# One core: features of phi(q) reordered, kv and M in groups of six heads, M's rows moved by DMA, and the first five tiles reordered

## The chip, the cores and the metric

The kernel runs on one core of one Trainium2 chip. The metric is the device time of one execution in microseconds (us). Before the change the median of three runs is 114.61 us (114.52 to 114.76). Engines are called as the profile calls them: PE (TensorE matmuls), PEld (its weight loads), DVE (VectorE), ACT (ScalarE), POOL (GpSimd), SP (SyncE, which issues most DMAs). `q`, `k`, `g` and `o` units are explained below.

## The reference, cut to what matters

```python
# S = 2048 tokens, D = 640 features, H = 32 heads of 20, F = 1536, C = 8; all bf16
xn = layernorm(x)                          # both branches read xn
# branch A: linear attention
q, k, v = split(xn @ wqkv)                 # per head: [S, 20]
phi = lambda t: where(t > 0, t + 1, exp(t)) + 1e-6
kv  = einsum("bhsd,bhse->bhde", phi(k), v) # per head 20 x 20
z   = sum over tokens of phi(k)
num = einsum("bhqd,bhde->bhqe", phi(q), kv)
den = phi(q) . z + 1e-6                    # one number per token and head
A   = (num / den) @ wo
# branch B: mixture of depths
r   = xn @ w_r;  idx = the 8 tokens with the largest r
y   = ((silu(xs @ w_gate) * (xs @ w_up)) @ w_down) * sigmoid(r[idx])   # xs = xn[idx]
B   = xn + scatter_add(idx, y)
out = x + A + B
```

## The kernel before

**Algebra.** v is never formed. With G = xn^T phi(k) (640 x 640), the kernel takes from wv^T G only the 20 x 20 blocks on the diagonal (that is kv, transposed), multiplies them by wo into one matrix M = blockdiag(kv) wo (640 x 640), and computes A = (phi(q) / den) M. The division is a multiplication of phi(q)^T (`pqT`, features on partitions, tokens along the row) by 1/den, which has to be spread from one row per head to the 20 rows of the head's features.

**Order.** All engines run an order written out by hand (`manual_schedule`): the order of the statements is the order on each engine's queue, and the framework only adds waits. 16 token tiles of 128 rows are used.

- *First five tiles* (L291 to L382): the mean and variance of tile t in two halves on DVE (`ln_stats`, L163, L166, L167), the inverse root on POOL (L169, L172; some 0.75 us, off DVE) or with root="A" as Ln and Exp on ACT (L176, L177), the scaling to xn on DVE (`ln_scale`, L181), five PE transposes (`turn_pe`, L193) and copies of the transposed tile out of PSUM (`turned`, L201 on ACT, L203 on DVE). Tiles 5 and later are transposed by DMA (`turn_dma`, L206). Seven matmuls on zeros and some short ones run ahead (`warm`, L292).
- *Loop over tiles 4 to 15* (L463 to L485): a k unit (`k_mm`, ten matmuls of 320 columns, L211), a q unit (`q_mm`, five matmuls of 512 columns, L245; 20 of them, unit u is feature chunk u mod 5 of 512 tokens) and a g unit (`g_mm`, five of 512 columns, L272). ACT takes Exp and Relu of each (`k_act` L227 to L229, `q_act` L257, L258), DVE joins them to phi (L234, L264). Weights and the x + xn store to a DRAM buffer (`xxd`) are issued by SP meanwhile.
- *Middle* (L492 to L783): z (L503), the top-8 search on DVE, the rest of G (`grest_mm`, L281), den of the first 1024 tokens (`den_mm`, L579; `den_act`, L590, L591), kv (`kv_mm`, L628: ten blocks of 64 columns, five matmuls each; masked by L640), M (`m_mm`, L655: four matmuls for each of five row chunks; copied by L666 or L668), the expert branch (`gu_mm` L693, L748, L756, ending in `y_sb`, L763, which POOL adds into `xxd` by an indirect DMA, L766), and the last seven q units. 1/den of the first half is written to DRAM (L620) and read back, each row 20 times, by 13 DMAs (`spread_dma`, L686); DVE multiplies five chunks of pqT by it (`scale_0`, L778). The sums x + xn + y come back by `reload` (L772).
- *Output stage* (L830 to L868): per token tile an o unit (`o_mm`, L810, ten matmuls of 320 columns over five feature chunks), `o_add` on DVE (L820) and a store (L827). Inside tiles 1 to 5 den of the second half is formed and spread on PE (`spread_mm`, L596: four matmuls for each of five chunks, in three places), copied by ACT (`spread_copy`, L610) and multiplied in by DVE (`scale_by`, L615).

PSUM has eight banks, given out by hand as the number in each call.

Of the kernel before, what the change touches and what calls it, by code (L numbers as in the profile page):

```python
# [21 lines left out]
NB = 10  # L22
EB = 80
DB = 64
# [13 lines left out]
def block_start(b):  # L38

    return DH * ((DB * b) // DH)  # L40


@with_exitstack
def kernel(
# [24 lines left out]
    evq = ctx.enter_context(tc.tile_pool(name="evq", bufs=2))  # L69
# [14 lines left out]
    wo_sb = sb([EB, NB, D], BF16, "wo_sb")  # L84
# [6 lines left out]
    grep = sb([P, D], BF16, "grep")  # L91
    headg = sb([P, KC, H], BF16, "headg")
# [11 lines left out]
    maskkv = sb([EB, 5, DB], BF16, "maskkv")  # L104
# [3 lines left out]
    kvT = sb([EB, NB, DB], BF16, "kvT")  # L108
# [3 lines left out]
    rdd = dram.tile([H, HALF], BF16, tag="rdd", name="rdd")  # L112
# [21 lines left out]
    nc.gpsimd.memset(grep[:], 1.0)  # L134

    def grep_rows(j, then=None):
        g = grep[32 * j : 32 * j + 32, :]
        nc.gpsimd.affine_select(
            out=g, in_=g, compare_op=ALU.is_ge, fill=0.0, base=0,
            pattern=[[1, D]], channel_multiplier=-DH,  # L140
        )
        if then is not None:
            then()
        nc.gpsimd.affine_select(
            out=g, in_=g, compare_op=ALU.is_ge, fill=0.0, base=DH - 1,
            pattern=[[-1, D]], channel_multiplier=DH,
        )
# [5 lines left out]
    grep_rows(0, late_x3)  # L153
# [88 lines left out]
    def q_mm(u, b, lo=0, hi=KC):  # L242
        m, tb = QU[u]
        for kc in range(lo, hi):
            nc.tensor.matmul(  # L245
                ps[:, b, :],
                lhsT=wq_sb[:, kc, m * P : (m + 1) * P],
                rhs=xnT[:, kc, tb * TBLK : (tb + 1) * TBLK],
                start=(kc == 0), stop=(kc == KC - 1),
            )  # L250
# [58 lines left out]
    warm(6, P)  # L309
# [3 lines left out]
    warm(4, P)  # L313
    turned(0, 7, "V", 0, 2)
    turned(0, 7, "A", 2, KC)
    ln_stats(2, "a")
# [6 lines left out]
    turned(1, 4, "A", 0, 2)  # L323
# [10 lines left out]
    ln_stats(2, "b")  # L334
    ln_stats(3)
    ln_scale(2)
    k_mm(1, 2, 0, 8)
    turn_pe(2, 7)
    k_mm(1, 2, 8)
# [3 lines left out]
    for b in range(5):  # L343
        nc.tensor.matmul(
            ps[0:EB, 4, b * DB : (b + 1) * DB],
            lhsT=grep[0:H, block_start(b) : block_start(b) + EB],
            rhs=grep[0:H, b * DB : (b + 1) * DB],
            start=(b == 0), stop=True, skip_group_check=True,
        )
    nc.scalar.copy(  # L350
        maskkv[:], ps[0:EB, 4, 0 : 5 * DB].rearrange("p (b f) -> p b f", b=5)
    )
    k_phi(0)
    k_mm(2, 5)
    ln_scale(3)
    turn_pe(3, 7)
    turned(3, 7, "A", 0, 2)
    turned(3, 7, "A", 2, KC)
    k_phi(1)
    g_mm(0)  # L360
    k_act(2, 5)
    ln_stats(4)
    ln_stats(5, "a")
# [3 lines left out]
    ln_stats(5, "b")  # L367
# [10 lines left out]
    ln_stats(7)  # L378
    ln_scale(6)
    turn_dma(6)  # L380
    q_mm(0, 7)
    k_phi(3)  # L382
    q_act(0, 7)

    def const_piece(i):
        if i == 0:
# [3 lines left out]
                pattern=[[P, KC], [-DH, H]], channel_multiplier=1,  # L390
            )
            nc.gpsimd.affine_select(
                out=headg[:], in_=headg[:], compare_op=ALU.is_ge, fill=0.0, base=DH - 1,
                pattern=[[-P, KC], [DH, H]], channel_multiplier=-1,
# [4 lines left out]
        elif i < 4:  # L399
            grep_rows(i)  # L400
# [37 lines left out]
    def load_wo(h):  # L438
        b0 = 5 * h
        src = bass.AP(  # L440
            tensor=A_wo.tensor, offset=A_wo.offset + HW * h * D,
            ap=[[D, EB], [3 * DH * D, 5], [1, D]],
        )
        nc.sync.dma_start(wo_sb[:, b0 : b0 + 5, :], src)
# [56 lines left out]
    def z_mm(t):  # L501
        for i in range(4):
            nc.tensor.matmul(  # L503
                ps[32 * i : 32 * i + 32, 6, 0 : KC * 32].rearrange("p (k f) -> p k f", k=KC),
                lhsT=ones_bf[:],
                rhs=pk[:, t, :].rearrange("p (k i f) -> p i k f", k=KC, i=4)[:, i, :, :],
                start=(t == 0), stop=(t == T - 1),
                tile_position=(0, 32 * i),
            )
# [21 lines left out]
    nc.scalar.copy(zs[:], ps[:, 6, 0 : KC * 32])  # L531
# [31 lines left out]
    for i in range(C):  # L563
# [5 lines left out]
        out=zm[:], in0=zT[:].rearrange("p (k h) -> p k h", k=KC), in1=headg[:], op=ALU.mult  # L569
# [24 lines left out]
    def spread_mm(h, m, half_bank):  # L594
        for j in range(4):
            nc.tensor.matmul(  # L596
                ps[:, j, 256 * half_bank : 256 * half_bank + 256],
                lhsT=grep[32 * j : 32 * j + 32, m * P : (m + 1) * P],
# [5 lines left out]
    spw = big.tile([P, 2, 4, 256], BF16, tag="wk_sb", name="spw")  # L604
    nsp = [0]

    def spread_copy(h, m, half_bank):
        w = spw[:, nsp[0] % 2, :, :]
        nsp[0] += 1
        nc.scalar.copy(w, ps[:, 0:4, 256 * half_bank : 256 * half_bank + 256])  # L610
        return w

    def scale_by(h, m, w):
        dst = pqT[:, m, h * HALF : (h + 1) * HALF].rearrange("p (j f) -> p j f", j=4)
        nc.vector.tensor_tensor(out=dst, in0=dst, in1=w, op=ALU.mult)  # L615
# [3 lines left out]
    for j in range(4):  # L619
        nc.sync.dma_start(  # L620
            rdd[:, 256 * j : 256 * j + 256], rdens[0][32 * j : 32 * j + 32, :]
        )

    def kv_mm(b0, b1, bank, base):
        for b in range(b0, b1):
            s0 = block_start(b)
            for c in range(KC):
                nc.tensor.matmul(  # L628
                    ps[0:EB, bank, (b - base) * DB : (b - base + 1) * DB],
                    lhsT=wv_sb[:, c, s0 : s0 + EB],  # L630
                    rhs=GT[:, c, b * DB : (b + 1) * DB],
                    start=(b == base and c == 0), stop=(c == KC - 1),
# [3 lines left out]
    def kv_mask(b0, b1, bank):  # L636
        b = b0
        while b < b1:
            e = min(b1, 5 * (b // 5) + 5)
            nc.vector.tensor_tensor(  # L640
                out=kvT[:, b:e, :],
                in0=ps[0:EB, bank, (b - b0) * DB : (e - b0) * DB].rearrange(
                    "p (b f) -> p b f", f=DB
                ),
                in1=maskkv[:, b % 5 : b % 5 + e - b, :], op=ALU.mult,
            )
            b = e
# [4 lines left out]
    def m_mm(m, b):  # L652
        for h in range(2):
            for j in range(2):
                nc.tensor.matmul(  # L655
                    ps[DB * j : DB * j + DB, b + h, 0:HW],
                    lhsT=kvT[:, 2 * m + j, :],
                    rhs=wo_sb[:, 2 * m + j, h * HW : (h + 1) * HW],
                    start=True, stop=True,
                    tile_position=(0, DB * j),  # L660
                )

    def m_copy(m, b, by_act=False):
        dst, src = M_sb[:, m, :].rearrange("p (b f) -> p b f", b=2), ps[:, b : b + 2, 0:HW]
# [4 lines left out]

    rsp = late[:, (T - 8) * D : (T - 8) * D + KC * HALF].rearrange("p (k f) -> p k f", k=KC)

    def spread_dma(m):
        f = m * P
        while f < (m + 1) * P:
            h, i = divmod(f, DH)
            n = ((m + 1) * P - f) // DH if i == 0 else 0
            if n:
# [217 lines left out]
```

## Time and profile before

| what | value |
|---|---|
| median of three runs | 114.61 us |
| the profiled execution's own time | 114.76 us |
| its span | 112.9 us |
| PE matmul busy | 106.7 us, 917 instructions |
| DVE busy | 84.6 us, 182 instructions |
| ACT busy | 59.3 us, 124 instructions |
| POOL busy | 32.1 us, 86 instructions |
| DMA | 23.25 MB, mean 206 GB/s |
| granted PE clock | 0.999 |

A row of the timeline gives start, duration, engine, source line, operation, output and inputs, shapes and count, and in brackets the idle time just before it with what ended it. A row of the chain of waits gives start, length and the engine and line that held the end of the program at that moment.

### The profile page before, as it was taken

How to read it: one execution, taken by the hardware profiler on the slowest of the kernel's cores; microseconds unless marked ns; L12 is line 12 of the kernel's file. 1: busy time of each engine (PE TensorE's matmuls, PEld its weight loads, DVE VectorE, ACT ScalarE, POOL GpSimd, SP SyncE). 2: the span in 40 equal slices, each digit the busy share in tenths (PEclk: the TensorE clock that was granted, in tenths of full speed). 3: DMA queues.
4: the chain of work that ended last, by engine and by line, in shares of the span. 5: the costliest groups of instructions: out<-in, count | busy, mean ns of one | idle time of the engine just before them, and what ended most of it. 6: DMA issues, size and time to landing. Idle time of an engine off the chain costs nothing.

```text
span 112.9 us, 2523 instructions
## 1 busy us (share of the span) xinstructions
PE 106.7 (94%) x917; PEld 63.6 (56%) x926; DVE 84.6 (75%) x182; ACT 59.3 (53%) x124; POOL 32.1 (28%) x86
## 2 busy tenths in 40 slices
PE   5999998999999999999999999999997999999990
PEld 2477563555555555555555589555334565777770
DVE  0787968988988898997888944348989568685580
ACT  1458819855686556865568542253885366300000
POOL 7405133278779788620000013100600000000000
PEclk9999999999999999999999999999999999999999
DMA  3999922324999969999972999023546927973333
GB/s 92 319 289 339 378 99 54 62 58 73 314 186 192 259 221 287 380 344 217 385 274 95 235 385 330 7 86 134 151 113 174 338 95 195 319 278 128 116 116 116
DMA packets 23410, 23.25 MB, mean 206 GB/s; under 512 B 8902, under 2 KB 21478, under 8 KB 23398
## 3 DMA queue, kind: packets, MB, share of 16 engines
q1 hardware_dynamic: 21420, 21.03, 64.8%
q10 hardware_dynamic: 1834, 2.02, 5.3%
q0 software_dynamic: 144, 0.04, 0.6%
q8 instruction: 7, 0.11, 0.4%
q14 instruction: 5, 0.04, 0.2%
HBM read 15.93 MB, written 5.35 MB: 189 GB/s over the span
## 4 chain that ended last, share of the span: by engine, by line
PE 86%; DVE 6%; issue 3%; ACT 2%; POOL 0%; ACTq 0%; DVEq 0%; POOLq 0%
PE ps L211 20%; PE ps L245 17%; PE ps L272 15%; PE ps L810 14%; PE ps L292 4%; PE ps L281 4%; DVE xn L820 2%; PE ps L628 2%; PE ps L693 2%; DVE pqT L778 1%; PE ps L193 1%; PE ps L655 1%; PE ps L579 1%; DVE pqT L264 1%; PE ps L503 1%
## 5 line engine op out<-in xcount | busy, mean ns | idle before, releaser
L211 PE MATMUL ps<-wk_sb,xnT 128*128 128x320 bf16 (+1 forms) x160 | 25.1, 300 | 0.0
L245 PE MATMUL ps<-xnT,wq_sb 128*128 128x512 bf16 x94 | 23.9, 379 | 0.9 <-ACT xnT L201 0.4
L810 PE MATMUL ps<-late,pqT 128*128 128x320 bf16 (+2 forms) x165 | 22.8, 295 | 0.6 <-DVE pqT L778 0.6
L211 PEld LDWEIGHTS <-xnT 128*128 128x128 bf16 x160 | 15.3, 98 | 8.6 <-issue 0.4
L272 PE MATMUL ps<-pk,xn 128*128 128x512 bf16 x77 | 19.7, 379 | 0.2
L810 PEld LDWEIGHTS <-pqT 128*128 128x128 bf16 x165 | 15.5, 98 | 7.4 <-DVE pqT L778 0.9
L227 ACT ACTIVATE ek<-ps 128x640 bf16<-128x640 f32 x16 | 11.3, 706 | 13.9 <-PE ps L211 13.9
L820 DVE TENSOR_TENSOR xn<-ps,x_sb 128x640 bf16<-128x640 f32 (+3 forms) x18 | 13.1, 747 | 6.0 <-PE ps L810 6.0
L257 ACT ACTIVATE eq<-ps 128x512 bf16<-128x512 f32 x20 | 12.3, 617 | 7.9 <-PE ps L245 7.8
L245 PEld LDWEIGHTS <-wq_sb 128*128 128x128 bf16 x100 | 9.3, 97 | 10.3 <-issue 1.7
L264 DVE SCALAR_TENSOR_TENSOR pqT<-eq,rq 128x512 bf16<-128x512 bf16 x20 | 13.7, 684 | 0.9 <-ACT rq L258 0.9
L234 DVE SCALAR_TENSOR_TENSOR pk<-ek,rk 128x640 bf16<-128x640 bf16 x16 | 12.9, 807 | 1.7 <-ACT rk L228 1.7
L272 PEld LDWEIGHTS <-xn 128*128 128x128 bf16 x80 | 7.6, 98 | 8.6
L258 ACT ACTIVATE rq<-ps 128x512 bf16<-128x512 f32 x20 | 12.3, 616 | 0.0
L181 DVE TENSOR_SCALAR xn<-x_sb,mv,rs 128x640 bf16<-128x640 bf16 x16 | 8.6, 536 | 3.9 <-POOL rs L172 3.6
L228 ACT ACTIVATE rk<-ps 128x640 bf16<-128x640 f32 x16 | 11.2, 702 | 0.0
L172 POOL TENSOR_TENSOR rs<-rs,half 128x1 f32<-128x1 f32 x14 | 10.7, 763 | 1.1
L169 POOL TENSOR_TENSOR rs<-mv,half 128x1 f32<-128x1 f32 x14 | 5.7, 409 | 15.6 <-DVE mv L167 15.5
L163 DVE BATCH_NORM_STATS2 st<-x_sb 128x6 f32<-128x320 bf16 x16 | 7.6, 472 | 3.2 <-DMA x_sb<-in_A_x_dram 3.2
L565 POOL COPY xsT<-xnT 128x5 bf16 x8 | 1.6, 206 | 21.6 <-DVE junk L714 18.1
L166 DVE BATCH_NORM_STATS2 st<-x_sb 128x6 f32<-128x320 bf16 x16 | 7.6, 475 | 0.0
L187 DVE TENSOR_TENSOR x_sb<-x_sb,xn 128x640 bf16<-128x640 bf16 x16 | 6.9, 477 | 0.0
(122 smaller groups left out, 101.1 us busy)
## 6 DMA issues: line engine op xcount, KB each, us to landing
x_sb<-in_A_x_dram SPq DMA_DIRECT2D x6, 320.0 KB
wg_sb<-in_B_w_gate_dram SPq DMA_DIRECT2D x5, 384.0 KB
wu_sb<-in_B_w_up_dram SPq DMA_DIRECT2D x5, 384.0 KB
wd_sb<-in_B_w_down_dram SPq DMA_DIRECT2D x3, 640.0 KB
xxd<-x_sb SPq DMA_DIRECT2D x2, 640.0 KB
out_dram<-xn SPq DMA_DIRECT2D x8, 160.0 KB
x_sb<-xxd SPq DMA_DIRECT2D x2, 640.0 KB
out_dram<-xn ACTq DMA_DIRECT2D x7, 160.0 KB
```

The source lines that it names most:

```text
L172: nc.gpsimd.tensor_tensor(out=rs[:, 1:2], in0=rs[:, 0:1], in1=half[:, 1:2], op=ALU.pow)
L211: nc.tensor.matmul(ps[:, b + h, 0:w], lhsT=xnT[:, kc, t * P : (t + 1) * P], rhs=wk_sb[:, kc, h * HW : h * HW + w], start=(kc == 0), stop=( ...
L227: nc.scalar.activation(e[:], ps[:, b : b + 2, 0:HW], AF.Exp)
L228: nc.scalar.activation(r[:], ps[:, b : b + 2, 0:HW], AF.Relu)
L234: nc.vector.scalar_tensor_tensor(out=pk[:, t, :].rearrange("p (b f) -> p b f", b=2), in0=e[:], scalar=1.0, in1=r[:], op0=ALU.min, op1=ALU.add,
L245: nc.tensor.matmul(ps[:, b, :], lhsT=wq_sb[:, kc, m * P : (m + 1) * P], rhs=xnT[:, kc, tb * TBLK : (tb + 1) * TBLK], start=(kc == 0), stop ...
L257: nc.scalar.activation(e[:], ps[:, b, :], AF.Exp)
L258: nc.scalar.activation(r[:], ps[:, b, :], AF.Relu)
L264: nc.vector.scalar_tensor_tensor(out=pqT[:, m, tb * TBLK : (tb + 1) * TBLK], in0=e[:], scalar=1.0, in1=r[:], op0=ALU.min, op1=ALU.add,)
L272: nc.tensor.matmul(ps[:, c, :], lhsT=xn[:, t, c * P : (c + 1) * P], rhs=pk[:, t, 0:512], start=(t == 0), stop=(t == T - 1),)
L810: nc.tensor.matmul(ps[:, b, 0 : c1 - c0], lhsT=pqT[:, kc, t * P : (t + 1) * P], rhs=M_sb[:, kc, c0:c1], start=(kc == 0), stop=(kc == KC - 1),)
L820: nc.vector.tensor_tensor(out=xn[:, t, c0:c1].rearrange("p (b f) -> p b f", f=w), in0=ps[:, b : b + n, 0:w], in1=x_sb[:, t, c0:c1].rearran ...
```

## The change

It has five parts.

1. **Features of phi(q).** The weights of q unit m were columns 128m to 128m+127 of wq; now they are columns 5p + m for p = 0 to 127, a view with a step of five elements. Row p of every chunk m then belongs to head p // 4, so one spread of 1/den (`gbig`, a 0/1 matrix) serves all five chunks. z is brought into the same order: its matmuls read contiguous columns, and the copy `zs` reorders them.
2. **The first half of the tokens** is divided like the second: `spread_mm(0)` (four matmuls) and one `spread_copy` of 1024 columns on ACT, then five multiplications. The DRAM detour (4 writes, 13 reads) is gone. For the second half there is one spread and one copy where there were five.
3. **kv and M** go by groups of six heads (five groups of 120 columns and one of 40): kv takes 30 matmuls (50 before), M 12 matmuls of up to 120 rows (20 of 64 rows in pairs before). The mask comes from POOL instead of five matmuls and an ACT copy in the first tiles.
4. **M's rows** must follow the order of the features, so each group is copied to `M_nat` (ACT four, DVE two) and one DMA on SP moves it: 120 rows go to 24 partitions with five rows each.
5. **First five tiles.** Tile 2's first half-statistics stand ahead of the copy of tile 0, its second half and an ACT root ahead of the copy of tile 1; tile 4's transposes stand behind k unit 3 with all of g unit 2 behind them; tile 5's statistics move behind them; two short warming matmuls go.

The diff, cut to its core:

```diff
-    warm(6, P)
+    warm(4, P)
     ln_scale(0)
     ln_stats(1, "b", root="A")
     turn_pe(0, 7)
     warm(4, P)
+    ln_stats(2, "a")
     turned(0, 7, "V", 0, 2)
     turned(0, 7, "A", 2, KC)
-    ln_stats(2, "a")
     ln_scale(1)
...
-    turned(1, 4, "A", 0, 2)
+    ln_stats(2, "b", root="A")
+    turned(1, 4, "V", 0, 2)
     turned(1, 4, "A", 2, KC)
...
-    ln_stats(2, "b")
-    ln_stats(3)
     ln_scale(2)
-    k_mm(1, 2, 0, 8)
+    ln_stats(3, "a")
+    k_mm(1, 2, 0, 4)
     turn_pe(2, 7)
-    k_mm(1, 2, 8)
+    k_mm(1, 2, 4)
...
-    for b in range(5):
-        nc.tensor.matmul(
-            ps[0:EB, 4, b * DB : (b + 1) * DB],
-            lhsT=grep[0:H, block_start(b) : block_start(b) + EB],
...
     k_mm(3, 5)
-    g_mm(2, 0, 3)
     turn_pe(4, 7)
-    g_mm(2, 3)
+    g_mm(2)
     turned(4, 7, "A", 0, 2)
     turned(4, 7, "A", 2, KC)
+    ln_stats(5)
     ln_scale(5)
...
-                lhsT=wq_sb[:, kc, m * P : (m + 1) * P],
+                lhsT=wq_sb[:, kc, :].rearrange("p (f m) -> p m f", m=KC)[:, m, :],
...
-    def spread_mm(h, m, half_bank):
+    def spread_mm(h):
         for j in range(4):
             nc.tensor.matmul(
-                ps[:, j, 256 * half_bank : 256 * half_bank + 256],
-                lhsT=grep[32 * j : 32 * j + 32, m * P : (m + 1) * P],
+                ps[:, j, 0:256],
+                lhsT=gbig[32 * j : 32 * j + 32, j * P : (j + 1) * P],
                 rhs=rdens[h][32 * j : 32 * j + 32, :],
...
+    def spread_copy(h):
+        nc.scalar.copy(spw[:, h, :, :], ps[:, 0:4, 0:256])
...
+    def kv_mm(g0, g1, bank):
+        for g in range(g0, g1):
+            f0, w = group(g)
             for c in range(KC):
                 nc.tensor.matmul(
+                    ps[0:w, bank, (g - g0) * GB : (g - g0) * GB + w],
+                    lhsT=wv_sb[:, c, f0 : f0 + w],
+                    rhs=GT[:, c, f0 : f0 + w],
...
+    def m_mm(g, b):
+        w = group(g)[1]
         for h in range(2):
+            nc.tensor.matmul(
+                ps[0:w, b + h, 0:HW],
+                lhsT=kvT[0:w, g, 0:w],
+                rhs=wo_sb[0:w, g, h * HW : (h + 1) * HW],
...
+    def m_out(g, b, by_act=False):
...
+        nc.sync.dma_start(M_sb[f0 // KC : (f0 + w) // KC, :, :], nat)
...
-    kv_mm(0, 8, 4, 0)
-    kv_mask(0, 8, 4)
-    for t in range(9, T):
+    kv_mm(0, 4, 4)
+    kv_mask(0, 4, 4)
+    for t in range(9, 11):
         grest_mm(t, 0, 4, 7)
+    spread_mm(0)
+    spread_copy(0)
+    for t in range(11, T):
+        grest_mm(t, 0, 4, 7)
...
-    for m in range(KC):
-        spread_dma(m)
...
-    MID = {1: den_1, 2: lambda: spread_1(0, 1), 4: lambda: spread_1(2, 3)}
-    END = {2: lambda: reload(8, 12), 4: lambda: reload(12, 16), 5: lambda: spread_1(4)}
+    MID = {1: den_1, 2: spread_1}
+    END = {2: lambda: reload(8, 12), 4: lambda: reload(12, 16)}
```

Three places show how instructions stand now. Names with a number are buffers of one tile: st, mv and rs hold statistics, mean with variance, and root; the pairs ek, rk and eq, rq hold Exp and Relu. Source lines differ by two to thirty between the kernels.

DVE in the first tiles, from the copy of tile 0's first two blocks on, before:

```order
L203 COPY xnT<-ps 128x2x128
L163 BN_STATS st_183<-x_sb 128x6
L181 TENSOR_SCALAR xn<-x_sb,mv_157,rs_158 128x640
L166 BN_STATS st_183<-x_sb 128x6
L167 BN_AGGR mv_184<-st_183 128x2
L163 BN_STATS st_220<-x_sb 128x6
L166 BN_STATS st_220<-x_sb 128x6
L167 BN_AGGR mv_221<-st_220 128x2
L181 TENSOR_SCALAR xn<-x_sb,mv_184,rs_185 128x640
```

and now, from tile 2's first half on:

```order
L161 BN_STATS st_180<-x_sb 128x6
L201 COPY xnT<-ps 128x2x128
L179 TENSOR_SCALAR xn<-x_sb,mv_158,rs_159 128x640
L164 BN_STATS st_180<-x_sb 128x6
L165 BN_AGGR mv_181<-st_180 128x2
L201 COPY xnT<-ps 128x2x128
L179 TENSOR_SCALAR xn<-x_sb,mv_181,rs_182 128x640
L161 BN_STATS st_220<-x_sb 128x6
```

Tile 2's statistics (st_183 before, st_180 now) have moved ahead of the copy out of bank 7, and tile 3's (st_220) behind tile 2's scaling; tile 1's first two blocks are now copied by DVE.

DVE between the expert branch's activations and the output stage, before (y_sb closes the expert branch):

```order
L750 COPY late<-ps 128x384
L264 SCALAR_TENSOR_TENSOR pqT<-eq_1267,rq_1268 128x512
L668 CAST late<-ps 128x640
L763 TENSOR_SCALAR y_sb<-ps,gcol 128x160
L668 CAST late<-ps 128x640
L264 SCALAR_TENSOR_TENSOR pqT<-eq_1336,rq_1337 128x512
L778 TENSOR_TENSOR pqT<-pqT,late 128x1024
L264 SCALAR_TENSOR_TENSOR pqT<-eq_1412,rq_1413 128x512
L778 TENSOR_TENSOR pqT<-pqT,late 128x1024
```

and now:

```order
L742 COPY late<-ps 128x384
L262 SCALAR_TENSOR_TENSOR pqT<-eq_1308,rq_1309 128x512
L754 TENSOR_SCALAR y_sb<-ps,gcol 128x160
L607 TENSOR_TENSOR pqT<-pqT,spw 128x1024
L262 SCALAR_TENSOR_TENSOR pqT<-eq_1377,rq_1378 128x512
L607 TENSOR_TENSOR pqT<-pqT,spw 128x1024
L262 SCALAR_TENSOR_TENSOR pqT<-eq_1388,rq_1389 128x512
L262 SCALAR_TENSOR_TENSOR pqT<-eq_1399,rq_1400 128x512
```

The copies of M are gone from this stretch, and of the five multiplications three stand ahead of it; the last one stood behind the last but one phi, and stands now behind the second.

ACT in the output stage, where the rows are the reciprocal of den (ld, rd), the stores that ACT issues and the copies of the spread, before:

```order
L590 ACTIVATE ld_1513<-ps,eps_100 128x256
L591 ACTIVATE rd_1514<-ld_1513 128x256
L827 DMA out_dram<-xn 128x640
L610 CAST spw<-ps 128x1024 x2
L827 DMA out_dram<-xn 128x640
L610 CAST spw<-ps 128x1024 x2
L827 DMA out_dram<-xn 128x640
L610 CAST spw<-ps 128x1024
```

and now:

```order
L588 ACTIVATE ld_1470<-ps,eps_100 128x256
L589 ACTIVATE rd_1471<-ld_1470 128x256
L805 DMA out_dram<-xn 128x640
L603 CAST spw<-ps 128x1024
L805 DMA out_dram<-xn 128x640 x6
L805 DMA out_dram<-xn 128x192
```

Four of five copies are gone, and with them the sixteen matmuls that fed them on PE.

More of the change, by code (lines that the diff above doesn't have):

```diff
@@ L617 @@
     den_mm(0, 6)
     den_act(0, 6)
[L619 to L626, printed above, removed]
+    def kv_mm(g0, g1, bank):
+        for g in range(g0, g1):
+            f0, w = group(g)
             for c in range(KC):
                 nc.tensor.matmul(
[L629 to L632, printed above, removed]
+                    ps[0:w, bank, (g - g0) * GB : (g - g0) * GB + w],
+                    lhsT=wv_sb[:, c, f0 : f0 + w],
+                    rhs=GT[:, c, f0 : f0 + w],
+                    start=(g == g0 and c == 0), stop=(c == KC - 1),
@@ L649, with kv_mask, kv_mask5 @@
+    def kv_mask(g0, g1, bank):
+        n = g1 - g0
+        nc.vector.tensor_tensor(
+            out=kvT[:, g0:g1, :],
+            in0=ps[0:GB, bank, 0 : n * GB].rearrange("p (g f) -> p g f", f=GB),
+            in1=mask2.unsqueeze(1).to_broadcast([GB, n, GB]), op=ALU.mult,
+        )
+    def kv_mask5(bank):
+        w = group(5)[1]
+        nc.vector.tensor_tensor(
+            out=kvT[0:w, 5, 0:w], in0=ps[0:w, bank, GB : GB + w], in1=mask2[0:w, 0:w],
+            op=ALU.mult,
+        )
     late = big.tile([P, T * D], BF16, tag="pk", name="late")
@@ L650 @@
     M_sb = late[:, 0 : KC * D].rearrange("p (k d) -> p k d", k=KC)
-    def m_mm(m, b):
+    M_nat = big.tile([P, KC, D], BF16, tag="wk_sb", name="M_nat")
+    def m_mm(g, b):
+        w = group(g)[1]
         for h in range(2):
[L654 to L661, printed above, removed]
```

243 lines of the change are left out of this document (103 added, 140 removed).

## The prediction

> **What bounds the kernel now.** I read the page's busy shares first, then the chain of waits in order of time, then the timeline at the places where the chain leaves PE.
>
> ```profile
> span 112.9 us, 2523 instructions
> PE 106.7 (94%) x917; PEld 63.6 (56%) x926; DVE 84.6 (75%) x182; ACT 59.3 (53%) x124; POOL 32.1 (28%) x86
> PE 86%; DVE 6%; issue 3%; ACT 2%; POOL 0%; ACTq 0%; DVEq 0%; POOLq 0%
> ```
>
> PE holds 86% of the chain. So the change is worth the PE time that it removes plus the PE waits that it ends, unless another engine takes over. The profiled execution took 114.76 us, its span is 112.9, and 1.86 us lie around it and stay. The median of the runs shown is 0.15 us lower, and I take that off at the end.
>
> The PE waits and the PE work that the change touches lie in three stretches. First tiles, in the chain:
>
> ```profile
> 10.39 0.30 PE ps L344 x5
> ...
> 16.70 0.29 PE ps L193 x5
> ...
> 17.01 0.76 ACT xnT L201 x2
> ...
> 19.06 1.51 PE ps L211 x10
> ```
>
> and one row of the timeline:
>
> ```profile
> 17.82 1.24 PE L245 MATMUL ps<-xnT,wq_sb 128*128 128x512 bf16 x5 [0.41 <-ACT xnT L201]
> ```
>
> L344 makes the mask. At 17.0 ACT empties bank 7 of tile 4, and q unit 0, which writes that bank, waits. From the first k unit of the loop (19.06) to the middle the chain stays on PE at 3.54 us a tile (k 1.38, q 1.08, g 1.08).
>
> Middle, chain:
>
> ```profile
> 25.19 1.08 PE ps L272 x5
> 26.27 1.38 PE ps L211 x10
> ...
> 67.33 1.65 PE ps L628 x40
> 68.98 2.46 PE ps L281 x44
> ...
> 73.44 0.50 PE ps L628 x10
> ...
> 74.87 0.39 PE ps L655 x4
> ...
> 79.82 1.19 PE ps L245 x5
> ```
>
> Output stage, chain, and one row of the timeline that shows the wait at its start:
>
> ```profile
> 86.90 0.99 PE L810 MATMUL ps<-late,pqT 128*128 128x320 bf16 x6 [0.58 <-DVE pqT L778]
> ```
>
> ```profile
> 86.90 0.99 PE ps L810 x6
> 87.89 0.66 PE ps L579 x20
> 88.55 1.47 PE ps L810 x10
> 90.02 0.33 PE ps L596 x8
> ...
> 95.96 0.29 PE ps L596 x4
> ```
>
> The first o unit waits for DVE's last multiplication of the first half. Later PE waits before the third spread (L596), whose banks the ACT copy of the second still holds.
>
> **Part A, first tiles.** Mask: 0.30 us of PE go. Its replacement on POOL runs inside the loop, where POOL has idle time. Bank 7: q unit 0 waited 0.41 us; behind the transposes stood two g matmuls of 0.22 us, now five (1.08 us by the row at 25.19), and ACT's copies need 0.76 us from the end of the transposes. 0.76 is under 1.08, so the wait goes. Sum -0.71.
>
> What the reordering could cost, by the rows of the same engines:
>
> ```profile
> 6.10 0.29 ACT L176 ACTIVATE rs<-mv,half 128x1 f32<-128x1 f32 x1 [1.11 <-DVE mv L167]
> 6.40 0.29 DVE L203 COPY xnT<-ps 128x256 bf16<-128x256 bf16 x1 [0.34 <-PE ps L193]
> 6.42 0.20 ACT L177 ACTIVATE rs<-rs 128x1 f32<-128x1 f32 x1
> 6.61 0.48 DVE L163 BATCH_NORM_STATS2 st<-x_sb 128x6 f32<-128x320 bf16 x1
> 8.09 0.75 ACT L201 COPY xnT<-ps 128x256 bf16<-128x256 bf16 x2 [0.77 <-PE ps L193]
> 8.74 0.71 ACT L227 ACTIVATE ek<-ps 128x640 bf16<-128x640 f32 x1
> ```
>
> DVE was idle for 0.34 us before the copy at 6.40. Half a set of statistics (0.48, some 0.1 of it overlapping the next) fits in with under 0.1 us left over, if tile 2 has landed by 6.0. At 6.61 it had, since no DMA wait stands there; so this costs 0 to 0.6, and I take 0. On ACT, Ln and Exp of tile 2's root now stand ahead of tile 1's copy. ACT was idle for 0.77 us there. Mean and variance are ready some 1.1 us after the scaling that begins near 6.7, at about 7.8; the root is done 0.5 later, at 8.3. ACT then copies three blocks, not five (DVE has the other two), and ends near 8.9, as now at 8.84. k unit 2 needs the banks of k unit 0 at 10.4, and the three ACT reads that begin then end at about 10.3. Queued behind the root on ACT are that copy and these reads, and k unit 1's second half waits for the copy only from 9.5. So the slack is 0.1 us, and I take no cost. DVE has the statistics of tiles 5 and 7 later than before, so that phi of tile 4 may come up to 0.4 us late for its g unit. Taken -0.7; bounds 0 to -0.85.
>
> **Part B, middle.** kv: 50 matmuls took 1.65 + 0.50 = 2.15 us, 0.041 each at 64 columns with weights of 80. Now 25 have 120 columns with weights of 120, and five 40 by 40. The nearest rows bound one of the 25: 0.056 (44 of 128 columns in 2.46) and 0.062 (0.041 times 120/80); five small ones at 0.041. 1.6 to 1.75, taken 1.7: -0.45. M: five units at 0.39 = 1.95 before, now 12 matmuls at the k unit's 0.138 = 1.66: -0.29. Spread of the first half on PE: half of the 0.33 that eight took, 0.17 to 0.33, taken 0.2. Sum -0.55.
>
> A rule speaks against this part. The Trainium skill (TensorE: Matmul & The Clock Gate, Weight-path perf modes) has the fast weight load only for weights of all 128 columns, and its section on LDWEIGHTS gives columns / 1.2 ns otherwise, 100 ns at 120 columns. If that were the pace, kv would take 2.7 us, Part B would come to about +0.45, and the whole to 112.5. The trace agrees that 80 columns load slower than 128, but not with the pace:
>
> ```profile
> L245 PEld LDWEIGHTS <-wq_sb 128*128 128x128 bf16 x100 | 9.3, 97 | 10.3 <-issue 1.7
> L628 PEld LDWEIGHTS <-wv_sb 128*80 128x80 bf16 x50 | 2.1, 120 | 0.5 <-issue 0.3 <-DMA wd_sb<-in_B_w_down_dram 0.2
> ```
>
> 120 ns for 80 columns stands against 97 ns for 128, yet the matmuls behind them went every 41 ns.
>
> Other engines in this stretch, by a row of the windows (stretch, length, then PE, PEld, DVE, ACT, POOL busy), one of the timeline and one of the groups:
>
> ```profile
> 71.44:76.79 5.35, 5.14 (x67) 2.44 (x69) 1.69 (x4) 2.82 (x6) 0.20 (x1) 1.00 0.20 61
> ```
>
> ```profile
> 75.16 0.56 DVE L744 TENSOR_TENSOR late<-ps,late 128x384 bf16<-128x384 f32 x1 [0.90 <-ACT late L742]
> ```
>
> ```profile
> L666 ACT CAST late<-ps 128x640 bf16<-128x640 f32 x2 | 1.4, 700 | 0.0
> ```
>
> ACT gains here one spread copy (1.01 us, in the row of L610 below), the GT copy that DVE had, and four copies of M at 0.70, two of which stand behind the expert branch's Exp; with 2.82 of 5.35 us busy it takes them in its idle time. DVE gains three multiplications (0.68, row L615 below) ahead of the expert product at 75.16; it was idle for 0.90 there and for most of the four us before, so y_sb, and with it the reload, stay at the same distance behind kv. SP has six DMAs in place of 4 + 13, behind the weights of w_down and ahead of the reloads. The last waits for ACT's copy of the last group, some 76.5 on the old clock, 8 us before the first o unit at 85. No row shows a DMA of this form; it costs nothing up to 8 us.
>
> **Part C, output stage.** Spread on PE: 0.33 + 0.33 + 0.29 = 0.95 before, once 0.2 now: -0.75. The second 0.33 is the spread of chunks 2 and 3, eight matmuls like the first. The wait at 86.90 (0.58, and 0.16 of refilling, since six matmuls took 0.99 and not 0.83) ends if DVE is no longer late. From 77 on DVE had seven phis, five multiplications, three copies of M; now seven phis and two multiplications. ACT is next: Exp and Relu of a q unit take 1.08 us start to start (84.20 to 85.28 below), as long as the unit on PE, so phi of the last unit ends some 2.0 us after PE has finished it; den needs it after one o unit and four matmuls (1.93 us) and four of its own five chunks (0.53): 0.45 us to spare. -0.74. The third spread's wait, 0.32 between the sixteen o matmuls' end at 95.64 and 95.96, goes with that spread. Sum -1.81.
>
> ```profile
> L610 ACT CAST spw<-ps 128x1024 bf16<-128x1024 f32 x5 | 4.9, 1014 | 3.7 <-PE ps L596 2.5 <-DVE xn L820 1.2
> L615 DVE TENSOR_TENSOR pqT<-pqT,spw 128x1024 bf16<-128x1024 bf16 x5 | 3.4, 682 | 0.9 <-ACT spw L610 0.9
> ```
>
> ```profile
> 84.20 0.60 ACT L257 ACTIVATE eq<-ps 128x512 bf16<-128x512 f32 x1 [0.49 <-PE ps L245]
> 84.41 2.33 SPq L772 DMA_DIRECT2D x_sb<-xxd  x5
> ...
> 85.28 0.60 ACT L257 ACTIVATE eq<-ps 128x512 bf16<-128x512 f32 x1
> ...
> 87.39 0.82 DVE L820 TENSOR_TENSOR xn<-ps,x_sb 128x640 bf16<-128x640 f32 x1
> ```
>
> DVE does one sum and one multiplication for each of tiles 2 to 6, 0.82 + 0.68 with some 0.14 of overlap, against 1.38 of PE: level.
>
> **The sum.** 114.76 - 0.70 - 0.55 - 1.81 = 111.7; less 0.15 for the median, 111.5 us.
>
> **Rivals.**
>
> *Strided weights (slower).* The q weights now step five elements, and no row of before has such a load. It took 97 ns, hidden behind a 216 ns matmul (1.08 / 5). There are 100 of them, so the 3.1 us gained are gone at 216 + 31 = 247 ns, 2.5 times the row. At three times (291) it is +7.5: 119 us. Against it: that is a long way from 97, and the slowest load in the rows, 120 ns for 80 columns, makes 192 for 128, still hidden. The Trainium skill (SBUF — State Buffer, The DMA port swizzle) lets bf16 step up to eight elements for free; no run here shows it.
>
> *The reload gates.* The reload was issued at 84.41, well behind the q units, and is as late on the new clock.
>
> ```profile
> 85.50:86.00 0.50, 0.50 (x6) 0.38 (x4) 0.50 (x2) 0.50 (x2) 0.00 (x0) 1.00 0.75 200
> 86.00:86.50 0.50, 0.33 (x3) 0.00 (x0) 0.50 (x2) 0.36 (x1) 0.00 (x0) 1.00 0.98 325
> ```
>
> The last number is GB/s: its bytes came from 85.5 on, so tile 0 landed near 86.5, at most by the sum at 87.39. On the old clock the third o unit wants that sum's bank at 87.7, and the sum takes 0.82. Landing at 87.39 costs 0.5: 112.0.
>
> *The first tiles give nothing.* Part A falls to 0 because DVE's or ACT's queue holds the next tile up as much as the bank did: 112.2.
>
> *Slow 120-column loads.* If a matmul of kv went at the 120 ns of the row above: 3.6 us against 1.7, 113.4.
>
> **How the numbers follow.** The forecast 0.60 (own range 110.8 to 112.1), first tiles give nothing 0.17, reload 0.10, slow loads 0.05, strided weights 0.08. All but the last are faster: a measurement here tells 0.2% (0.23 us) from no change, and only a strided price of just about 31 ns lands inside. Faster 0.90, same 0.02, slower 0.08. The range ends at 110.7, where three terms come in whole: 0.85 of Part A, kv at 1.6, and q units without the restart behind an M unit (1.19 at 79.82 against 1.08; up to five times, so 0.5), and at 113.0, beyond the reload and the first tiles together.
>
> **What would show it.** Right: L344's place gone and no ACT wait before q unit 0; kv near 1.7 us; one spread in the output stage; no DVE wait in the first o unit; q units still 1.08 us. Wrong: q units longer than 1.08 in the loop; PE idle on DMA before the first o unit (M's rows) or on DVE's sums (reload); a DVE or ACT wait in front of k units 1, 2 or 4, or g unit 4.

## The result and the profile after

| what | before | after |
|---|---|---|
| median of 14 runs each, the same chip | 114.76 us (114.51 to 115.42) | 114.0 us (113.44 to 116.03) |
| ratio, 95% interval | | 0.9929 [0.9907, 0.9951] |
| the profiled execution's own time, its span | 114.76, 112.9 us | 113.98, 112.3 us |

One of the 14 runs after (116.03), one of only_first and one of ahead went at a mean granted clock of 0.983 to 0.985, where every other run had 0.995 or more, and the ratios and the medians further down leave these three out.

The changed kernel is 0.7% faster. The forecast was 111.5 us, with a range that ended at 113.0: the side was right and the size was not. The page's first lines and the shares of the chain, after:

```profile
span 112.3 us, 2409 instructions
PE 104.6 (93%) x879; PEld 65.0 (58%) x879; DVE 82.3 (73%) x181; ACT 58.8 (52%) x124; POOL 29.5 (26%) x81
PE 75%; DVE 10%; POOL 5%; DMA 4%; issue 1%; ACT 1%; SPq 1%; DVEq 0%; POOLq 0%
```

PE's work fell by 2.1 us, and the span by only 0.6. The chain says where the rest is: PE held 86% of it before and holds 75% now, while DVE went from 6% to 10%, and POOL and DMA, which held nothing, have 5% and 4%.

The chain in order of time shows in which part of the program they stand. First the first tiles and the loop, after (start, length, engine and line):

```profile
1.72 4.74 DMA x_sb<-in_A_x_dram
...
10.60 0.41 DVE st L164
...
11.33 0.66 POOL rs L167
...
12.06 0.58 POOL rs L170
...
```

From 10.60 on, the second half-statistics of tile 3, POOL's two steps and then the scaling (at 12.67) stand in a row on the chain. Before, PE held this stretch nearly throughout. The middle and the output stage of the same chain:

```profile
68.89 1.24 PE ps L617 x20
...
70.58 0.22 PE ps L594 x4
...
72.02 0.82 PE ps L650 x6
...
73.73 0.27 PE ps L650 x2
...
74.93 0.64 PE ps L617 x10
...
76.50 0.79 PE ps L650 x4
...
80.13 6.17 PE ps L243 x28
86.30 1.90 PE ps L788 x14
88.20 0.66 PE ps L577 x20
...
90.32 0.22 PE ps L594 x4
90.54 17.24 PE ps L788 x126
```

From 80.13 to the end of the last o unit PE runs with no wait. Two stretches can be cut out of the two kernels with the same borders: from the start of the kernel to the first kv matmul, and from there to the end of PE's last piece.

| stretch | before | after | difference |
|---|---|---|---|
| first kv matmul at | 67.33 | 68.89 | +1.56 |
| from there to the end of the last o unit | 41.26 (to 108.59) | 38.89 (to 107.78) | -2.37 |

The second row is Parts B and C of the prediction, for which it gave -0.55 and -1.81, together -2.36; that the two agree to 0.01 us is luck, as the terms of Part B show below. The first row is Part A and the loop, for which it gave -0.70. The tail behind PE is 0.2 us longer. So one part failed, by 2.3 us, and it is the first tiles. The timeline there, after:

```profile
6.48 0.49 DVE L161 BATCH_NORM_STATS2 st<-x_sb 128x6 f32<-128x320 bf16 x1 [0.46 <-DMA x_sb<-in_A_x_dram]
6.89 0.27 DVE L201 COPY xnT<-ps 128x256 bf16<-128x256 bf16 x1
7.22 1.00 PE L209 MATMUL ps<-wk_sb,xnT 128*128 128x320 bf16 x6 [1.11 <-DVE xnT L201]
12.67 0.45 DVE L179 TENSOR_SCALAR xn<-x_sb,mv,rs 128x640 bf16<-128x640 bf16 x1 [0.74 <-POOL rs L170]
13.90 1.24 PE L270 MATMUL ps<-pk,xn 128*128 128x512 bf16 x5 [0.28 <-DVE pk L232]
16.30 0.45 DVE L179 TENSOR_SCALAR xn<-x_sb,mv,rs 128x640 bf16<-128x640 bf16 x1 [0.72 <-POOL rs L170]
16.80 0.45 PE L191 MATMUL ps<-ident,xn 128*128 128x128 bf16 x5 [0.28 <-DVE xn L179]
19.30 1.55 PE L209 MATMUL ps<-wk_sb,xnT 128*128 128x320 bf16 x10
21.60 0.45 DVE L179 TENSOR_SCALAR xn<-x_sb,mv,rs 128x640 bf16<-128x640 bf16 x1 [0.71 <-POOL rs L170]
24.35 0.45 DVE L179 TENSOR_SCALAR xn<-x_sb,mv,rs 128x640 bf16<-128x640 bf16 x1 [0.72 <-POOL rs L170]
25.75 0.77 DVE L232 SCALAR_TENSOR_TENSOR pk<-ek,rk 128x640 bf16<-128x640 bf16 x1
26.58 1.24 PE L270 MATMUL ps<-pk,xn 128*128 128x512 bf16 x5 [1.11 <-DVE pk L232]
```

and the same places before:

```profile
6.75 1.02 PE L211 MATMUL ps<-wk_sb,xnT 128*128 128x320 bf16 x6
19.02 1.54 PE L211 MATMUL ps<-wk_sb,xnT 128*128 128x320 bf16 x10
22.84 0.77 DVE L234 SCALAR_TENSOR_TENSOR pk<-ek,rk 128x640 bf16<-128x640 bf16 x1
```

Read from top to bottom, this is the account of the 1.56 us. DVE waits 0.46 for tile 2's rows of x, and the copy of tile 0 stands behind that: k unit 0 starts 0.47 later. The mask (0.30) and the wait for bank 7 (0.41) are gone, as forecast. Two new waits of PE, 0.28 each, stand at g unit 1 (for phi) and at the transposes of tile 4 (for the scaling). A row's length runs some 0.16 past the start of the next unit (1.24 for five matmuls that follow each other in 1.08), so from start to start each of these waits is longer: 0.57 at bank 7, 0.45 at each of the two new ones. A gap of 0.21 before g unit 0 is gone too. 0.47 - 0.30 - 0.57 - 0.21 + 0.90 = 0.29, and k unit 4, the first of the loop, is 0.28 late. Then g unit 4 waits for phi of tile 4, 1.11 us by its row and 1.27 from start to start, and is 1.56 late; nothing afterwards moves it.

Why phi is late, by a row of the waits (total, times, longest), after:

```profile
DVE xn L179 <- POOL rs L170: 6.5, 11, 0.9
```

and before:

```profile
DVE xn L181 <- POOL rs L172: 3.6, 7, 0.9
```

Before, the statistics of tiles 3 and 7 and the first half of tile 5's stood ahead of the previous tile's scaling, and POOL took the root while DVE did something else. In the changed order they stand behind it. (Part 5 moves more than its list and the cut diff show: tile 7's statistics go behind phi of tile 3 and tile 6's scaling, and tile 3's transposes behind phi of tile 1 and g unit 0.) So tiles 3 and 7 lost the lead of their own statistics, and tiles 4 and 6 lost the neighbour's statistics that had filled the time of their root. At each of these four DVE now waits for POOL, 0.74, 0.72, 0.71 and 0.72, in all the 2.9 us by which the two rows differ; at tile 5 it waited 0.93 before as well. Everything queued behind the scaling on DVE, phi among it, waits with it.

### The profile page after: what moved, and what is told of

Read it like the earlier page. It is cut to its first block, busy times and chain, and to the rows that moved or that the text cites. A ratio compares the mean times of both kernels' runs of the same rounds, so it can differ in the third digit from the quotient of the medians.

```text
span 112.3 us, 2409 instructions
## 1 busy us (share of the span) xinstructions
PE 104.6 (93%) x879; PEld 65.0 (58%) x879; DVE 82.3 (73%) x181; ACT 58.8 (52%) x124; POOL 29.5 (26%) x81
## 4 chain that ended last, share of the span: by engine, by line
PE 75%; DVE 10%; POOL 5%; DMA 4%; issue 1%; ACT 1%; SPq 1%; DVEq 0%; POOLq 0%
PE ps L788 18%; PE ps L243 17%; PE ps L209 14%; PE ps L270 12%; DMA x_sb<-in_A_x_dram 4%; PE ps L279 4%; POOL rs L170 3%; POOL rs L167 2%; DVE xn L179 2%; DVE st L164 2%; PE ps L617 2%; PE ps L650 2%; PE ps L671 2%; DVE st L161 1%; DVE xn L798 1%
## 5 line engine op out<-in xcount | busy, mean ns | idle before, releaser
L788 PE MATMUL ps<-late,pqT 128*128 128x320 bf16 (+2 forms) x165 | 22.3, 295 | 0.0
L243 PEld LDWEIGHTS <-wq_sb 128*128 128x128 bf16 x100 | 11.5, 118 | 8.0 <-issue 0.3
L167 POOL TENSOR_TENSOR rs<-mv,half 128x1 f32<-128x1 f32 x13 | 7.2, 551 | 20.2 <-DVE mv L165 18.6
L179 DVE TENSOR_SCALAR xn<-x_sb,mv,rs 128x640 bf16<-128x640 bf16 x16 | 7.1, 446 | 6.5 <-POOL rs L170 6.5
L170 POOL TENSOR_TENSOR rs<-rs,half 128x1 f32<-128x1 f32 x13 | 10.2, 781 | 1.0
```

The lines of the kernel that those rows point to most:

```text
L170: nc.gpsimd.tensor_tensor(out=rs[:, 1:2], in0=rs[:, 0:1], in1=half[:, 1:2], op=ALU.pow)
L243: nc.tensor.matmul(ps[:, b, :], lhsT=wq_sb[:, kc, :].rearrange("p (f m) -> p m f", m=KC)[:, m, :], rhs=xnT[:, kc, tb * TBLK : (tb + 1) * T ...
L788: nc.tensor.matmul(ps[:, b, 0 : c1 - c0], lhsT=pqT[:, kc, t * P : (t + 1) * P], rhs=M_sb[:, kc, c0:c1], start=(kc == 0), stop=(kc == KC - 1),)
```

## The experiments

Two theories stood against each other at first. *Lateness*: the order of the first tiles alone costs it, by the two places above, DVE's queue in front of k unit 0 and the statistics that lost their lead. *Layout*: the rest of the change (the new view of the weights, the mask on POOL, other buffers and loads) makes the first tiles late, and their order is innocent.

One number serves as a ruler in all of them: the start of g unit 4, and how much of the profiled execution's time lies behind it. The start of k unit 0 divides what lies ahead of it.

| kernel | start of k unit 0 | start of g unit 4 | its own time | time behind g unit 4 | median of its runs |
|---|---|---|---|---|---|
| before | 6.75 | 25.02 | 114.76 | 89.74 | 114.76 |
| only_first | 7.60 | 26.95 | 116.9 | 89.95 | 116.4 |
| after | 7.22 | 26.58 | 113.98 | 87.40 | 113.98 |
| x2_back | 6.50 | 25.91 | 113.41 | 87.50 | 113.5 |
| x2_back_act | 6.61 | 25.48 | 112.89 | 87.41 | 112.81 |
| ahead | 6.76 | 25.24 | 112.73 | 87.49 | 112.73 |
| both | 6.28 | 24.96 | 112.44 | 87.48 | 112.45 |
| old_first | 6.32 | 24.70 | 112.19 | 87.49 | 112.2 |
| old_turn4 | 6.76 | 24.61 | 112.01 | 87.40 | 111.98 |

The medians come from three sessions: the kernel before had 115.02 beside only_first, x2_back, ahead and old_first, and 114.93 beside the other three, with runs from 114.4 to 116.0. So a difference of under some 0.5 us between two rows is not shown by the medians alone; the columns of the traces carry it, for one execution each.

The seven kernels with the new middle and output stage agree within 0.1 us behind g unit 4, and stand 2.2 to 2.6 us below the two with the old ones. So the gain of those parts was delivered in full each time, and what tells the seven apart lies ahead of g unit 4.

### only_first: the kernel before, with the new order of the first tiles alone

```diff
 # before, with the statements of part 5 of the change; the mask's matmuls stay
+    ln_stats(2, "a")
     turned(0, 7, "V", 0, 2)
...
+    ln_stats(2, "b", root="A")
+    turned(1, 4, "V", 0, 2)
...
-    ln_stats(2, "b")
-    ln_stats(3)
     ln_scale(2)
+    ln_stats(3, "a")
```

> The kernel before with the change's new order of the first five tiles alone (the mask's matmuls stay, the features, kv, M and the spread are as before). Lateness theory: the new order itself costs 1.5 us, 0.5 by tile 2's arrival ahead of tile 0's copy and 1.1 by the statistics of tiles 5 and 7 that lost their lead, so 116.2 us, slower by 1.3%, with POOL waits before the scalings of tiles 3 to 7 and a wait of some 1 us before g unit 4. Layout theory (the new feature order, its step-5 weight loads or POOL's new pieces hold the loop's first tiles up): not slower than before, 114.0 to 114.8, since the wait for the bank before q unit 0 is gone.

Measured: 116.4 us (116.37 to 116.9), ratio to before 1.0109 [1.0018, 1.0199]. The waits of PE, of DVE for POOL, and the row where DVE's queue is stopped:

```profile
PE ps L211 <- DVE xnT L203: 1.4, 1, 1.4
PE ps L272 <- DVE pk L234: 1.1, 1, 1.1
DVE xn L181 <- POOL rs L172: 6.5, 11, 0.9
```

```profile
6.86 0.49 DVE L163 BATCH_NORM_STATS2 st<-x_sb 128x6 f32<-128x320 bf16 x1 [0.80 <-DMA x_sb<-in_A_x_dram]
```

The new order alone makes the old kernel slower, with the same three waits. Layout falls as the main cause: none of it is in this kernel. Tile 2's rows came even later here, and DVE waited 0.80 us. A late tile 2 is therefore not the layout's doing either: with the new layout it was there by 6.30 in x2_back, 6.14 in both and 6.18 in old_first, by statistics that began then without a wait.

### old_first: the change, with the old order of the first tiles

```diff
 # the change, with the statements of the first tiles as before, without the mask's matmuls
-    ln_stats(2, "a")
     turned(0, 7, "V", 0, 2)
     turned(0, 7, "A", 2, KC)
+    ln_stats(2, "a")
...
+    ln_stats(5, "b")
+    g_mm(2, 0, 3)
     turn_pe(4, 7)
-    g_mm(2)
+    g_mm(2, 3)
```

> The change with the old order of the first five tiles (and without the mask's matmuls there). Lateness theory: keeps the 2.4 us of the middle and output stage and the mask's 0.3: 112.0 us, ratio 0.976. Layout theory: no better than the change, 113.5 to 114.3, and g unit 4 still waits for phi.

Measured: 112.2 us (112.12 to 112.72), ratio 0.9758 [0.9686, 0.9829]. Lateness had 112.0, layout 113.5 to 114.3. The waits:

```profile
DVE xn L179 <- POOL rs L170: 2.3, 4, 0.9
PE ps L243 <- ACT xnT L199: 0.4, 1, 0.4
```

DVE's wait for POOL is down to 2.3 us, and the old wait for bank 7 is back. The new order of the first tiles cost 1.8 us in medians.

### x2_back: tile 2's first half-statistics back behind the copy of tile 0

```diff
-    ln_stats(2, "a")
     turned(0, 7, "V", 0, 2)
     turned(0, 7, "A", 2, KC)
+    ln_stats(2, "a")
```

> The change with tile 2's first half-statistics put back behind the copies of tile 0. Lateness theory: the first k unit starts 0.4 us sooner (near 6.8), everything behind follows as far as the chain through DVE and POOL starts there: 113.6 us. If the tile's arrival costs nothing because the later chain has slack: 114.0.

Measured: 113.5 us (113.41 to 114.22), ratio 0.9879 [0.9804, 0.9954]. The timeline:

```profile
6.03 0.28 DVE L201 COPY xnT<-ps 128x256 bf16<-128x256 bf16 x1
```

The copy starts at 6.03 where the change had it at 6.89. k unit 0 gains 0.72 of this (6.50; now it is the weights wk that come last, and PE waits 0.31 us for them), and g unit 4 has the other wait unchanged, 1.11 (at 25.91). So the first place is worth 0.5 us in medians and 0.57 between the profiled executions. The runs of the two kernels overlap, so the size rests on the traces.

### ahead: the statistics of tiles 5 and 7 a step earlier again

```diff
     ln_stats(4)
+    ln_stats(5, "a")
     g_mm(1)
     k_phi(2)
     ln_scale(4)
+    ln_stats(5, "b")
...
-    ln_stats(5)
     ln_scale(5)
...
     ln_stats(6)
-    k_phi(3)
+    ln_stats(7)
     ln_scale(6)
...
-    ln_stats(7)
     q_mm(0, 7)
+    k_phi(3)
     q_act(0, 7)
```

> The change with the statistics of tiles 5 and 7 put back to where they stood, half a tile to a tile ahead of the scaling, and phi of tile 3 behind tile 6's scaling again; tiles 2 and 3 as in the change. Lateness theory: the 1.1 us wait before g unit 4 goes, 112.9 us. If POOL's longer adds (0.65 us in place of 0.19) and not the order are the cause: 113.7 or more.

Measured: 112.73 us (112.55 to 113.38), ratio 0.9811 [0.9714, 0.9908]. The timeline and the waits:

```profile
6.02 0.49 DVE L161 BATCH_NORM_STATS2 st<-x_sb 128x6 f32<-128x320 bf16 x1
6.43 0.27 DVE L201 COPY xnT<-ps 128x256 bf16<-128x256 bf16 x1
```

```profile
DVE xn L179 <- POOL rs L170: 4.8, 9, 0.9
PE ps L270 <- DVE pk L232: 0.3, 1, 0.3
```

The wait at g unit 4 is gone (the 0.3 left is g unit 1's), and the kernel is 1.25 us under the changed one in medians. Not all of this is the edit's. In this execution tile 2 came in time, so that k unit 0 began at 6.76 and not at 7.22, 0.46 sooner, with the first place as it was. From k unit 0 to g unit 4 it is 18.48 us here and 19.36 in the changed kernel: 0.88 is what the second place is worth in this trace. The rival in the expectation, POOL's longer additions, is not separated from the order by this edit: with statistics beside them again, the additions of tiles 4, 6 and 7 took 0.20, 0.19 and 0.36 us where the changed kernel had 0.66, 0.59 and 0.46, 0.96 less of the 1.7 by which DVE's wait for POOL fell. The first two rows say something about the first place too: tile 2's statistics began at 6.02 without a wait, and the copy still began at 6.43, 0.4 later than in x2_back: the half-statistics are in the way by their own length even where nobody waits for a DMA.

### both: the two edits together

```diff
 # x2_back and ahead
```

> The change with both repairs: tile 2's first half-statistics behind the copies of tile 0, and the statistics of tiles 5 and 7 ahead again. Tile 2's root on ACT, its second half ahead of tile 1's copy, tile 3's halves around tile 2's copies and turn 4 behind k 3 stay as in the change. Lateness theory: the gains of the two repairs add, 0.5 + 0.9, so 112.6 us, and the spread of the runs narrows as tile 2's arrival no longer holds tile 0's copy. If the two repairs shorten the same wait: 113.0, as the second alone.

Measured: 112.45 us (112.44 to 112.64), ratio 0.9781 [0.9712, 0.9851]. That is 1.53 us under the changed kernel in medians, where the two edits alone gave 0.48 and 1.25, so each repair has its own effect, but the medians do not simply add up. The trace says why: k unit 0 begins 0.94 us sooner than in the changed kernel (6.28), and from there to g unit 4 it is 18.68 us, 0.68 less; the 1.25 of ahead held part of the first place already. Whether the spread of the runs narrows is not shown: it is 0.2 us here, but 0.8 in x2_back, which has the same repair of the first place.

### old_turn4: the old order, but tile 4's transposes behind k unit 3

This is the one idea in part 5 whose gain could be read from the profile of before, the wait for bank 7, put alone on top of old_first.

```diff
-    g_mm(2, 0, 3)
     turn_pe(4, 7)
-    g_mm(2, 3)
+    g_mm(2)
```

> The change with the old order of the first five tiles but tile 4's transposes behind k unit 3 and all of g unit 2 behind them, as the change has it. By Part A of the forecast the bank wait of 0.41 us before q unit 0 goes and nothing else moves: 111.8 us against 112.2 with the old order throughout. If k unit 4 only waits for ACT instead, no better than 112.2.

Measured: 111.98 us (111.67 to 112.05), ratio 0.9727 [0.9657, 0.9797], the best version here and faster than both kernels of the case. All that PE still waits for from another engine behind the warming:

```profile
PE ps L209 <- DVE xnT L201: 0.2, 1, 0.2
```

Against old_first that is 0.2 us, half of the 0.41 and too little for the medians to show; the trace shows that the wait for bank 7 is gone. The profiled execution of old_turn4 had a slower start, though. Its row for the first five transposes, and q unit 0:

```profile
5.63 0.74 PE L191 MATMUL ps<-ident,xn 128*128 128x128 bf16 x5
17.33 1.24 PE L243 MATMUL ps<-xnT,wq_sb 128*128 128x512 bf16 x5
```

In old_first the five transposes took 0.45 us, k unit 0 started at 6.32 (here at 6.76) and q unit 0 at 17.49. From k unit 0 to q unit 0 it is 10.57 here and 11.17 there, 0.6 us less: the 0.41 of the bank with the 0.16 by which its row is too short, as worked out above.

### x2_back_act: roots of tiles 3 and 4 on ACT

```diff
 # x2_back, and:
-    ln_stats(3, "b")
+    ln_stats(3, "b", root="A")
-    ln_stats(4)
+    ln_stats(4, root="A")
```

> The change with tile 2's first half-statistics put back, and the roots of tiles 3 and 4 by ACT (Ln, Exp, 0.5 us) and not by POOL (add and power, 1.2 us with phi on DVE beside it). If POOL's root stands in the chain of the first tiles: the scalings of tiles 3 and 4 come some 0.5 us sooner each, the wait before g unit 4 shrinks by 0.5 to 0.7, and 113.0 us against 113.5 without it. If only the order of DVE's instructions counts, or ACT's queue pays it back: 113.5 or more.

Measured: 112.81 us (112.72 to 113.19), ratio 0.9813 [0.9741, 0.9885]; 0.7 us under x2_back. The timeline:

```profile
11.68 0.32 ACT L174 ACTIVATE rs<-mv,half 128x1 f32<-128x1 f32 x1
12.27 0.45 DVE L179 TENSOR_SCALAR xn<-x_sb,mv,rs 128x640 bf16<-128x640 bf16 x1 [0.75 <-ACT rs L175]
15.09 0.44 DVE L179 TENSOR_SCALAR xn<-x_sb,mv,rs 128x640 bf16<-128x640 bf16 x1
```

It gains at one tile only. Tile 4's scaling comes at 15.09 (15.63 in x2_back), and the wait before its transposes (0.27 there) is gone; the one before g unit 4 went from 1.11 to 0.87, less than the 0.5 to 0.7 expected. Tile 3's is not sooner (12.27 against 12.01), since on ACT its Ln stood behind the reads of k unit 1 and began at 11.68. A faster engine for the root does less than statistics that have their lead: `both`, which leaves the roots of these tiles on POOL, is 0.36 us faster.

## Why the prediction was right and wrong

**The bound: right for the loop, the middle and the end.** A PE-bound stretch paid out what was taken from PE. It was no longer right for the first 27 us, where the change itself made DVE and POOL the bound.

**Part A, the failed step.** The terms that I took from PE's rows held: the mask's 0.30 and the bank's 0.41 are gone (old_turn4 shows no bank wait; from start to start it was 0.57). The costs that I set against them did not. Two sentences failed.

- "if tile 2 has landed by 6.0 ... so this costs 0 to 0.6, and I take 0." It cost 0.47 of PE's start in the profile, 0.5 in x2_back. I read the arrival from a row that came later in the queue (6.61, no DMA wait), which says only that the tile was there by 6.61, and in the profiles it came at up to 6.86. The 0.34 us of idle time into which I fitted the statistics was no room either: it existed since PE's five transposes took 0.74 us in that execution. With 0.45, as in the changed kernel, the copy could have started near 6.0, so that any length put in front of it shows. In old_first, whose transposes took 0.45 too, k unit 0 began at 6.32, so against an equal start the place cost 0.9.
- "phi of tile 4 may come up to 0.4 us late for its g unit." That phi of tile 4 began at 25.75 instead of 22.84, 2.9 us late, and g unit 4 lost about 1.3: the wait in front of g unit 4 that the prediction itself named as a sign of being wrong. I had treated POOL's root as "off DVE", which is how the profile of before shows it, because other statistics filled its time there. Moving them put POOL's two steps, 0.65 + 0.57 us in the chain for tile 3, between DVE's instructions at tiles 3, 4, 6 and 7, and phi of tile 4, queued behind all of them, inherits four waits of 0.7. I looked at the tile that was moved soonest (2), and not at the ones that paid for it.

My rival "the first tiles give nothing" had the right mechanism (the queue holds up the next tile) and the wrong floor. It ended at zero; the measured value is +1.56, outside the bounds of 0 to -0.85.

**Part B: the sum held, its terms less so.** kv start to first o unit took 17.75 us before (85.08 by the timeline) and 17.25 after (86.14): -0.50 against -0.55. kv took 1.24 + 0.64 = 1.88 (forecast 1.7), M 0.82 + 0.27 + 0.79 = 1.88 (forecast 1.66), the spread 0.22 (forecast 0.2): by these terms alone -0.12. The rest came from the term that I had kept for the end of the range: 28 matmuls of q in 6.17 us are 1.10 a unit, where before four units took 1.19 each, one behind the expert branch and three behind a piece of M, some 0.36 in all. So the size of the sum was right by two errors that nearly cancel. kv's thirty matmuls went every 63 ns, just above my upper bound of 62. The Trainium skill (TensorE: Matmul & The Clock Gate, LDWEIGHTS) would have a load of 120 columns take 100 ns; their weight loads took 134 ns in the rows, and yet the matmuls went at 63, so neither number is the pace at which they follow each other here, and kv took 1.88 us where 100 ns a load would have made it 2.7.

**Part C: right, term by term.** First o unit to the end of PE fell from 23.51 to 21.64, -1.87 against -1.81. Spread on PE 0.95 to 0.22; fourteen o matmuls in 1.90 with no wait in them; no wait at the one spread that is left.

**The rivals.** *Strided weights* fell: the load is slower, and hidden.

```profile
L243 PEld LDWEIGHTS <-wq_sb 128*128 128x128 bf16 x100 | 11.5, 118 | 8.0 <-issue 0.3
```

118 ns in place of 97, behind 216 ns of matmul, and q units still take 1.08 us. The Trainium skill (SBUF — State Buffer, The DMA port swizzle) calls a step of up to eight bf16 elements free; here it is not quite, by 21 ns a load, in this view. *The reload* fell too, as its issue and the first sum show:

```profile
84.49 2.33 SPq L763 DMA_DIRECT2D x_sb<-xxd  x5
88.06 0.82 DVE L798 TENSOR_TENSOR xn<-ps,x_sb 128x640 bf16<-128x640 f32 x1
```

The sum stands 3.6 us behind the issue with no DMA wait ahead of it. *Slow 120-column loads* (120 ns) fell with 63. M's DMAs, issued from 73.76 on, made no o unit wait.

**What the range lacked.** I gave 0.08 to the whole slower side, and let every mishap in the first tiles stop at zero gain. A part with an unknown arrival and a moved chain needs a bound on the loss side from its own rows: POOL's root (some 0.75 us by the rows of before) times the tiles whose root lost its cover, which for four tiles makes about the 2.9 us that phi came late.

## What to carry to other kernels

When statements are moved on an in-order engine, list every tile that loses distance between producer and consumer, not only the one that gains it: a latency that the profile shows as hidden on another engine is hidden by that distance and comes back with its full length. A row with no DMA wait says that the data was there by then, not when it came; work placed ahead of that moment waits for the transfer whenever it is late (three profiles had the tile by 6.02, at 6.48 and at 6.86), and a critical copy should not stand behind it. If a change has independent parts, time them apart: here one part gave 2.4 us and another took 1.6, and the sum looked like a change that does little.

## What the runs showed of the hardware that I had not expected

**POOL's small addition ends with the scaling or phi that DVE runs beside it.** The first step of the root, an addition on 128 x 1, took 0.19 us in some places of the first 31 us and 0.38 to 0.66 in others. From the kernel before, one beside a scaling (the DVE row, then POOL's), one beside statistics, one beside the phi that began at 22.84 (its row is shown above):

```profile
9.05 0.45 DVE L181 TENSOR_SCALAR xn<-x_sb,mv,rs 128x640 bf16<-128x640 bf16 x1
9.17 0.38 POOL L169 TENSOR_TENSOR rs<-mv,half 128x1 f32<-128x1 f32 x1 [0.15 <-DVE mv L167]
13.55 0.44 DVE L163 BATCH_NORM_STATS2 st<-x_sb 128x6 f32<-128x320 bf16 x1
13.72 0.19 POOL L169 TENSOR_TENSOR rs<-mv,half 128x1 f32<-128x1 f32 x1 [3.54 <-DVE mv L167]
23.01 0.66 POOL L169 TENSOR_TENSOR rs<-mv,half 128x1 f32<-128x1 f32 x1 [2.39 <-DVE mv L167]
```

The scaling ends at 9.50 and the addition at 9.55; phi ends at 23.61 and the addition at 23.67. Beside statistics it is done after 0.19, at 13.91, while they run to 13.99. The rows of the changed kernel read the same: phi from 11.16 to 11.93, the addition from 11.33 to 11.98. This looks like a lock that POOL waits for. The Trainium skill (SBUF — State Buffer, Who interferes with whom) states such a rule: VectorE and GpSimd share a pair of ports, held exclusively for a whole instruction, by VectorE instructions with two inputs in SBUF or in a two-port mode. The rows agree, for phi (two inputs) and for the scaling, and with the statistics, which have one. One row does not fit: at 19.80 of the kernel before, an addition that started 0.07 us after a scaling took 0.19 beside it. Perhaps it had the lock first; no row shows when a lock is taken, and no run moved phi alone to test it.

It bears on the miss: in the changed order phi of k or q follows directly on mean and variance at tiles 3, 4, 6, 7 and 8, where the additions took 0.46 to 0.66, and their mean between 9 and 30 us rose from 378 to 552 ns. So the lost cover seems to have cost twice: the root came into the chain, and it got longer there. What the second part is worth in time no run shows: ahead took away both together.

**The first transposes take 0.45 or 0.74 us** for the same five matmuls, in executions of kernels with the same statements there (old_first, old_turn4). All of PE is slower then, not the transposes alone: the four short warming matmuls behind them take 0.39 us in old_first and 0.63 in old_turn4. And all these executions begin slow: the first seven warming matmuls of 512 columns take 3.17 us in both, 0.45 each, where later ones follow each other every 0.216. So PE starts at about half its later pace, and the moment at which it changes differs from execution to execution, before the transposes in old_first and behind them in old_turn4. The granted clock of the profile does not show this; it reads 1.00 from the start in both. k unit 0 starts up to 0.4 us apart by it. A count of idle time in the first 7 us of one profile is good to no better than that.
